# A fused mLSTM and mixture-of-experts kernel on one core: the state product behind the next scores, half-height products in runs of eight, gate products over 128 rows

## The chip, the core and the metric

The kernel runs on one core of a Trainium2 chip. The metric is device microseconds of one execution; the median of three runs of the kernel before is 420.7 us. TensorE (PE in the profile) multiplies, VectorE (DVE), ScalarE (ACT) and GpSimd (POOL) do the elementwise work, SyncE (SP) issues the transfers. PE writes only PSUM, which has eight banks of 128 x 512 floats.

## The reference, cut to what matters

```
for t in range(S):                       # mLSTM, B=2, H=8, S=768, D=40
    m_new  = maximum(f + m, i)
    f_stab, i_stab = exp(f + m - m_new), exp(i - m_new)
    C = f_stab * C + i_stab * outer(v_t, k_t)
    n = f_stab * n + i_stab * k_t
    y[t] = sigmoid(o_t) * (C @ q_t) / maximum(abs(n . q_t), 1)
x = y as (1536, 320)
for e in range(4):                       # experts, F=1024, dense
    out += p[:, e] * (relu(x @ w1[e]) @ w2[e])
```

## The kernel before, in words

The first part computes the mLSTM in chunks of 128 steps, six for each of the two batches, numbered n = 0 to 11. A chunk has these parts on PE: `inter` (product of the carried state with q; L458), `intra` (masked scores times values; L473, two 64-column products side by side), `state` (the chunk's own contribution to the carried state; L430, two 40-column products side by side, none in chunks 5 and 11), `scores` of the next chunk (L412, two products of at most 64 rows side by side), and `turn` (transposes of the result; L500). ACT scales the product of `inter` into `yb` (L465), DVE does `norm` (L486 to L493), the state's sum (L440), `weigh` (L418) and the decay scans (L385), POOL scales keys and values and the carried state (L396, L401, L446). Between these parts the loop issues `steps` of expert 0 as fillers: a step is a block of layer 1 (L147) or one output block of layer 2 (L178 to L180) with its eviction (L183 on ACT, L185 on DVE from expert 1 on).

The tiles `y1` (inter), `y0` (intra), `st` (state) and `px` (turn) all come from the pool `ps_y` with two banks, in this order, so `st` takes the bank of `y1` once `yb` has read it.

The gates are prepared in the first 30 us. Three of their products have fewer than 128 rows: `gate_t` (L298, 48 rows), `gate_l` (L320, 16 rows) and `spread` (L368, 48 rows).

Experts 1 to 3 then run in three groups of 512 tokens each, nine groups in all. A group has eight blocks of layer 1 (seven products of 128 rows each, plus one product of 64 rows, L170) and four outputs of layer 2 (24 products each). The products of 64 rows are done in pairs, one on each half of PE's rows, four at a time: `corners` is called at f0 = 0 and f0 = 4 and opens four banks, taken in turn from six (`ps_l` four, `ps_h` two); the two banks of `ps_o` hold the outputs.

Nothing reorders the program: each engine runs its instructions in the order in which the code issues them.

Of the kernel before, what the change touches and what calls it, by code (L numbers as in the profile page):

```python
# [18 lines left out]
L = 128  # L19
# [10 lines left out]

TERMS = ((0, 0), (0, 3), (3, 0), (1, 1), (1, 4), (4, 1), (2, 2), (2, 5))

QUAD = 4
KX, KW = 5, 6
C = 64
WARM = 4
# [7 lines left out]
def tile_mlstm_moe(ctx, tc, gt, qk, vk, ot, dp, w1, w2, out):  # L44
# [58 lines left out]
        split_hi(ws[:, HI, f], raw[:, f])  # L103
        split_lo(ws[:, LO, f], ws[:, HI, f], raw[:, f], eng)

    xd, banks = [], []

    def next_bank():

        i = len(banks) % 6  # L110
        p, tag = (ps_l, "pl") if i < 4 else (ps_h, "ph")
        banks.append(p.tile([L, 1, 512], F32, tag=tag, name="ph"))
        return banks[-1]

    class Expert:


        def __init__(self, e, t0, n, w1s, w2s):
            self.e, self.t0, self.n, self.w1s, self.w2s = e, t0, n, w1s, w2s
            self.nf = 512 // n  # L120
            self.hs = []
            self.nh, self.no = NF // self.nf, n // L
            self.i = 0
            self.quad = []

        def step(self):
            i = self.i
# [7 lines left out]
        def hidden(self, f0):  # L135
            n, nf = self.n, self.nf
            terms = TERMS
            if self.e:
                if not self.quad:
                    self.corners(f0)  # L140
                ph, terms = self.quad.pop(0), TERMS[:-1]
            else:
                ph = ps_h.tile([L, nf, n], F32, tag="ph", name="ph")
            for i in range(nf):
                f = f0 + i
                for k, (xi, wi) in enumerate(terms):
                    nc.tensor.matmul(  # L147
                        ph[:, i, :],
                        self.w1s[:, wi, f * L:(f + 1) * L],
                        xst[:, xi, self.t0:self.t0 + n],  # L150
                        start=(k == 0 and not self.e),
                        stop=(k == len(terms) - 1),
                    )
            h = hps[-1].tile([L, 2, nf, n], F32R, tag="h", name="h")
            hh, hl = h[:, HI], h[:, LO]
            nc.scalar.activation(hh, ph, AF.Relu)  # L156
            nc.vector.scalar_tensor_tensor(  # L157
                out=hl, in0=ph, scalar=0.0, in1=hh.bitcast(F32), op0=ALU.max, op1=ALU.subtract
            )
            self.hs += [(hh[:, i, :], hl[:, i, :]) for i in range(nf)]  # L160

        def corners(self, f0):

            t = slice(self.t0, self.t0 + self.n)
            self.quad = [next_bank() for _ in range(QUAD)]
            for i, ph in enumerate(self.quad):
                f = slice((f0 + i) * L, (f0 + i + 1) * L)
                r = slice(C * (i % 2), C * (i % 2) + C)
                x = xd[0][r, t] if i % 2 else xst[r, 2, t]
                nc.tensor.matmul(ph[:, 0, :], self.w1s[r, 5, f], x, start=True, stop=False)  # L170

        def output(self, t):
            e, ws = self.e, self.w2s
# [19 lines left out]
    with ExitStack() as actx:  # L193
# [37 lines left out]
        fs = gp.tile([BH, S], F32, name="fs")  # L231
        bs = gp.tile([BH, NC, L], F32, name="bs")

        ib = gp.tile([48, S], F32, name="ib")
        fr = a1.tile([48, NPE * L], F32R, name="fr")
        f_d = dram.tile([BH, S], F32, name="f_d")
        ident = const.tile([L, L], F32, name="ident")
        id4 = const.tile([L, 4, L], F32, name="id4")
# [1 line left out]

        bl = const.tile([L, NC, B * NP], F32, name="bl")

        sel = const.tile([48, BH], F32R, name="sel")

        par = gp.tile([BH, 2], F32, name="par")
        even = gp.tile([BH, 2, 64], F32, name="even")
        pair = gp.tile([BH, B * NP], F32, name="pair")
        fc = fs.rearrange("p (c t) -> p c t", t=L)

# [41 lines left out]
        def gate_t(c0, c1):  # L291

            pit = pits[c0] = ps_y.tile([L, 512], F32, tag="y", name="pit")
            n = c1 - c0
            po = n * 48
            for c in range(c0, c1):
                o = (c - c0) * 48
                nc.tensor.matmul(  # L298
                    pit[:, o:o + 48], ib[:, c * L:(c + 1) * L], ident[0:48, 0:48],
                    start=True, stop=True,  # L300
                )
            nc.scalar.activation(
                ibT[:, c0:c1], pit[:, 0:po].rearrange("t (c g) -> t c g", c=n), AF.Copy
            )

        def gate_last(c0, c1):
            n, m = c1 - c0, B * NP
            last = lasts[c0] = gp.tile([BH, m, n], F32, tag=f"last{c0}", name="last")
            nc.gpsimd.tensor_mul(
                last, pair.unsqueeze(2).to_broadcast([BH, m, n]),  # L310
                gat[:, 0].rearrange("p (c t) -> p c t", t=L)[:, c0:c1, L - 1].unsqueeze(1)
                .to_broadcast([BH, m, n]),
            )
# [48 lines left out]

        def spread(n, pool, tag):

            b, c = n // NC, n % NC
            fbs[n] = [pool.tile([L, 4, L], F32, tag=tag, name="fb") for _ in range(2)]
            for h in range(H):
                nc.tensor.matmul(  # L368
                    fbs[n][h // 4][:, h % 4, :],
                    sel[:, b * H + h:b * H + h + 1].to_broadcast([48, L]),  # L370
                    fr[:, c * L:(c + 1) * L], start=True, stop=True,
                )

        def load_f(n):
# [45 lines left out]
        def state(n, pool=ps_y, tag="y"):  # L420

            c, vv, kk = n % NC, vvs[n], kp[n % 2]
            if c == NC - 1:
                return
            st = pool.tile([L, NP, L], F32, tag=tag, name="st")
            blocks = [(slice(64 * r, 64 * r + D), slice(64 * r, 64 * r + D + 1)) for r in range(2)]
            for p in range(NP):
                for r, (q, q2) in enumerate(blocks):
                    h = 2 * p + r
                    nc.tensor.matmul(  # L430
                        st[q, p, q2], kk[:, h, 0:D], vv[:, h, 0:D + 1], start=True, stop=True
                    )
            cout = cs[(c + 1) % 2]
            if c == 0:
                for q, q2 in blocks:
                    copy(nc.scalar, cout[q, :, q2], st[q, :, q2])
            else:
                cd = cds.pop(n)
                for q, q2 in blocks:
                    nc.vector.tensor_add(cout[q, :, q2], cd[q, :, q2], st[q, :, q2])  # L440
# [89 lines left out]
        load_w1(1)  # L530
        make_identity(nc, ident)
        nc.gpsimd.memset(ib, 0.0)
        for t in vp + kp:
            nc.gpsimd.memset(t, 0.0)
        nc.vector.memset(mb[:, 0:1], -1e30)
# [1 line left out]
        nc.vector.memset(bs, 0.0)  # L537
        for t in cs:
            nc.vector.memset(t, 0.0)
        nc.vector.tensor_add(sel, ident[0:48, 0:BH], ident[0:48, 32:32 + BH])  # L540
        nc.scalar.activation(id4, ident.unsqueeze(1).to_broadcast([L, 4, L]), AF.Copy)
        heads = ident[0:BH, 0:BH].rearrange("k (i r) -> k i r", r=2)
        nc.vector.tensor_reduce(
            out=par.unsqueeze(2), in_=heads.rearrange("k i r -> k r i"),
            axis=mybir.AxisListType.X, op=ALU.add,
        )
        nc.scalar.activation(even, par.unsqueeze(2).to_broadcast([BH, 2, 64]), AF.Copy)
        nc.vector.tensor_add(pair, heads[:, :, 0], heads[:, :, 1])
        gate_max(0, 2)
        gate_f(0, 2, nc.vector)  # L550
        gate_i(0, 2, nc.vector)
# [72 lines left out]
        for n in range(2, NCH):  # L624
            j, cc = n // 2, n % 2
            k = SLOTS[n - 2]
            nxt = n + 1 < NCH
            if cc == 0 and j + 1 < NG:
                load_qk(j + 1)
                load_vk(j + 1)  # L630
            if NPE < n + 2 < NCH:
                load_f(n + 2)
            if cc == 0:
                if j > 1:
                    gate_o(j)
                if j + 1 < NG:
                    load_o(j + 1)
            if nxt:
                decay(n + 1)
            steps(k[0])  # L640
            if n == 2:
                quarter_hi(2)
                quarter_lo(2)
            inter(n)
            if n == 3:
                weights_out(4, nc.gpsimd)
            intra(n)
            state(n)
            norm(n)
            if n == 2:  # L650
                quarter_hi(3)
                quarter_lo(3)
            if nxt:
                scores(n + 1)
                values(n + 1)
                keys(n + 1)
                weigh(n + 1)
                carry(n + 1)
            steps(k[1])
            if cc == 0:  # L660
                steps(k[2])
            turn(n)
            turn_lo(n)
            if cc == 1:
                steps(k[2])
            if n == 2:
                weights_out(0, nc.vector)

                psum_e = const.tile([L, NCH, 1], F32, name="psum_e")
                nc.vector.tensor_reduce(out=psum_e, in_=pw, axis=mybir.AxisListType.X, op=ALU.add)  # L670
                nc.vector.tensor_scalar_add(psum_e, psum_e, 1e-9)
                nc.vector.reciprocal(psum_e, psum_e)
                nc.vector.tensor_mul(pw, pw, psum_e.to_broadcast([L, NCH, NE]))
# [108 lines left out]
```

## Time and profile before

| | |
|---|---|
| median of 3 runs | 420.7 us (420.6 to 420.71) |
| the profiled execution's own time | 420.61 us |
| span of its instructions | 418.8 us |
| PE busy | 408.6 us (98% of the span) |
| PEld (weight loads) busy | 364.7 us (87%) |
| DVE / ACT / POOL busy | 178.9 / 125.0 / 81.0 us |
| chain that ended last | PE 91%, ACT 3%, DVE 2%, POOL 2% |

A row of the timeline gives the start in us, the time from its first start to its last end, the engine, the line, output <- inputs, the shapes and the count of merged instructions; in brackets stands the idle time before it and what ended it. PE records overlap (a product's record lasts longer than the distance to the next), so distances are taken from start to start. An fp32 product appears as two weight loads and two passes.

### The profile page before, as it was taken

Reading aid. Unit: us, or ns where it says so; the run is one execution under the profiler, and the core shown is the slowest. Engines: PE = TensorE matmul, PEld = TensorE weight load, DVE = VectorE, ACT = ScalarE, POOL = GpSimd, SP = SyncE. Lnnn points to the kernel's source line nnn. Section 1 sums busy time; section 2 is a strip of 40 time slices with the busy share of each in tenths; the row PEclk is TensorE's granted clock in tenths of the full one; section 3 lists DMA queues with packets and bytes.
Section 4 is the critical chain, followed back from the end, with each engine's and each line's share of the span. In section 5 each row is a group of like instructions: output and inputs, shape, how many; then the busy total and the mean of one; then the engine's idle time right before and its main releaser. Section 6 shows DMA issues by size and latency. Waiting matters only on the chain.

```text
span 418.8 us, 7140 instructions
## 1 busy us (share of the span) xinstructions
PE 408.6 (98%) x3026; PEld 364.7 (87%) x3026; DVE 178.9 (43%) x321; ACT 125.0 (30%) x298; POOL 81.0 (19%) x92
## 2 busy tenths in 40 slices
PE   9898999999999999999999999999999999999996
PEld 5698899988899997997987978979979879789796
DVE  8969778575846213313223133132142341231321
ACT  5666223433343434205113042043130230220210
POOL 6865601222200441103310010015100000000000
PEclk9999999999999999999999999999999999999999
DMA  7988617276000030400300004003000000001001
GB/s 202 273 276 217 183 52 205 74 188 239 2 2 2 2 125 2 150 2 0 127 0 2 0 2 150 2 2 113 13 0 2 0 2 36 28 0 49 16 16 49
DMA packets 15080, 29.34 MB, mean 70 GB/s; under 512 B 1000, under 2 KB 10728, under 8 KB 13736
## 3 DMA queue, kind: packets, MB, share of 16 engines
q1 hardware_dynamic: 15048, 28.88, 22.6%
q8 instruction: 24, 0.39, 0.4%
q14 instruction: 8, 0.07, 0.0%
HBM read 26.86 MB, written 2.02 MB: 69 GB/s over the span
## 4 chain that ended last, share of the span: by engine, by line
PE 91%; ACT 3%; DVE 2%; POOL 2%; issue 1%; POOLq 0%; ACTq 0%
PE ph L147 40%; PE po L178 13%; PE po L180 13%; PE po L179 13%; PE ph L170 3%; PE s L412 2%; PE y L473 2%; PE y L458 2%; PE st L430 1%; PE px L500 1%; POOL w2s L92 1%; ACT yb L465 1%; POOL w1s L92 0%; ACT L262 0%; ACT L358 0%
## 5 line engine op out<-in xcount | busy, mean ns | idle before, releaser
L147 PE MATMUL ph<-xst,w1s 128*128 128x512 f32 (+1 forms) x888 | 171.1, 349 | 0.0
L147 PEld LDWEIGHTS ph<-xst,w1s 128*128 128x128 f32 x888 | 140.2, 189 | 27.8 <-issue 6.6
L178 PE MATMUL po<-w2s,h 128*128 128x320 f32 x384 | 119.6, 311 | 0.2 <-POOL w2s L92 0.2
L156 ACT ACTIVATE h<-ph 128x512 fp32r<-128x512 f32 x96 | 57.4, 598 | 205.6 <-PE ph L147 205.0
L180 PE MATMUL po<-w2s,h 128*128 128x320 f32 x384 | 118.6, 309 | 0.0
L179 PE MATMUL po<-w2s,h 128*128 128x320 f32 x384 | 118.6, 309 | 0.0
L157 DVE SCALAR_TENSOR_TENSOR h<-ph,h 128x512 fp32r<-128x512 f32 x96 | 66.2, 690 | 116.2 <-ACT h L156 115.8
L178 PEld LDWEIGHTS po<-w2s,h 128*128 128x128 f32 x384 | 72.1, 188 | 1.4 <-POOL w2s L92 0.5
L179 PEld LDWEIGHTS po<-w2s,h 128*128 128x128 f32 x384 | 72.1, 188 | 0.4
L180 PEld LDWEIGHTS po<-w2s,h 128*128 128x128 f32 x384 | 72.1, 188 | 0.0
L185 DVE SCALAR_TENSOR_TENSOR acc<-po,pw,acc 128x320 f32<-128x320 f32 x36 | 19.8, 550 | 100.0 <-PE po L180 100.0
L92 POOL TENSOR_TENSOR w1s<-raw,w1s 128x512 fp32r<-128x512 f32 (+1 forms) x24 | 23.6, 1017 | 58.2 <-ACT w1s L89 58.2
L92 POOL TENSOR_TENSOR w2s<-raw,w2s 128x640 fp32r<-128x640 f32 x6 | 9.4, 1571 | 104.0 <-ACT w2s L89 104.0
L385 DVE TENSOR_TENSOR_SCAN dd<-fb,id 128x512 f32<-128x512 f32 x24 | 29.4, 1264 | 0.2
L183 ACT ACTIVATE acc<-po,pw 128x320 f32<-128x320 f32 x12 | 6.3, 528 | 43.1 <-PE po L180 43.1
L465 ACT ACTIVATE yb<-y,ibT 128x41 f32<-128x41 f32 x80 | 16.0, 311 | 3.9 <-PE y L458 3.9
L418 DVE TENSOR_TENSOR pm<-s,dd 128x512 f32<-128x512 f32 x24 | 15.4, 682 | 0.2
L401 POOL TENSOR_TENSOR kp<-vk,dd 128x320 f32<-128x320 f32 x10 | 7.4, 737 | 38.1 <-DVE dd L385 38.1
L473 PE MATMUL y<-vp,pm 128*64 128x41 f32 x384 | 13.8, 231 | 0.7 <-DVE xst L508 0.7
L412 PE MATMUL s<-qk 64*128 64x128 f32 (+1 forms) x192 | 14.1, 284 | 0.2 <-DVE pm L418 0.2
L473 PEld LDWEIGHTS y<-vp,pm 128*64 128x64 f32 x384 | 12.3, 138 | 2.2 <-issue 0.8
L89 ACT ACTIVATE w2s<-raw 128x640 fp32r<-128x640 f32 x12 | 8.8, 732 | 15.9 <-DMA raw<-in_w 15.9
(94 smaller groups left out, 252.5 us busy)
## 6 DMA issues: line engine op xcount, KB each, us to landing
raw<-in_w SPq DMA_DIRECT2D x3, 1536.0 KB, 6.9
fb<-f_d SPq DMA_DIRECT2D x8, 512.0 KB, 7.2
raw<-in_w SPq DMA_DIRECT2D x3, 1280.0 KB
qk<-in_qk SPq DMA_DIRECT2D x4, 832.0 KB
vk<-in_vk SPq DMA_DIRECT2D x4, 640.0 KB, 8.1
acc<-in_ot SPq DMA_DIRECT2D x6, 320.0 KB, 10.8
out<-acc SPq DMA_DIRECT2D x12, 160.0 KB, 1.8
qk<-in_qk SPq DMA_DIRECT2D x4, 416.0 KB
```

The source lines that it names most:

```text
L92: eng.tensor_sub(lo, raw, hi.bitcast(F32))
L147: nc.tensor.matmul(ph[:, i, :], self.w1s[:, wi, f * L:(f + 1) * L], xst[:, xi, self.t0:self.t0 + n], start=(k == 0 and not self.e), stop=( ...
L156: nc.scalar.activation(hh, ph, AF.Relu)
L157: nc.vector.scalar_tensor_tensor(out=hl, in0=ph, scalar=0.0, in1=hh.bitcast(F32), op0=ALU.max, op1=ALU.subtract)
L178: nc.tensor.matmul(po, hh[:, sl], ws[:, LO, f, :], start=(f == 0), stop=False)
L179: nc.tensor.matmul(po, hh[:, sl], ws[:, HI, f, :], start=False, stop=False)
L180: nc.tensor.matmul(po, hl[:, sl], ws[:, HI, f, :], start=False, stop=(f == NF - 1))
L185: nc.vector.scalar_tensor_tensor(out=acc[:, i, :], in0=po, scalar=pw[:, i, e:e + 1], in1=acc[:, i, :], op0=ALU.mult, op1=ALU.add,)
L385: nc.vector.tensor_tensor_scan(out=dds[n][:, 4 * i:4 * i + 4].rearrange("p h t -> p (h t)"), data0=fbs[n][i].rearrange("p h t -> p (h t)") ...
L412: nc.tensor.matmul(ss[n][r][:, p, :], kg[q, p], qg[q, p], start=True, stop=True)
L465: nc.scalar.activation(yb[:, h], y1[:, h, 0:D + 1], AF.Copy, scale=ibT[:, c, i:i + 1])
L473: nc.tensor.matmul(y[t, h, 0:D + 1], pms[n][:, h, t], vvs[n][:, h, 0:D + 1], start=True, stop=True,)
```

## The change

Three things change.

1. In the loop over chunks 2 to 10, `state(n)` is issued behind `norm(n)` and `scores(n + 1)` in place of ahead of them.
2. `corners` is called once a group. It opens eight banks (two of `ps_o`, four of `ps_l`, two of `ps_h`) and issues all eight products of 64 rows, blocks 2 to 7 first and blocks 0 and 1, which lie in the banks of `ps_o`, last.
3. `gate_t`, `gate_l` and the spreads of chunks 2 and 3 read 128 rows; the added rows are zero. The tiles `ib`, `fr`, `sel`, `par`, `even` and `last` are made 128 rows high, and two small clears of `last` on POOL are added.

```
-    def next_bank():
-        i = len(banks) % 6
-        p, tag = (ps_l, "pl") if i < 4 else (ps_h, "ph")
-        banks.append(p.tile([L, 1, 512], F32, tag=tag, name="ph"))
-        return banks[-1]
+    def hidden_banks():
+        pools = [(ps_o, "po")] * 2 + [(ps_l, "pl")] * 4 + [(ps_h, "ph")] * 2
+        return [p.tile([L, 1, 512], F32, tag=tag, name="ph") for p, tag in pools]
...
-                if not self.quad:
-                    self.corners(f0)
-                ph, terms = self.quad.pop(0), TERMS[:-1]
+                if f0 == 0:
+                    self.corners()
+                ph, terms = self.banks[f0], TERMS[:-1]
...
-        def corners(self, f0):
+        def corners(self):
             t = slice(self.t0, self.t0 + self.n)
-            self.quad = [next_bank() for _ in range(QUAD)]
-            for i, ph in enumerate(self.quad):
-                f = slice((f0 + i) * L, (f0 + i + 1) * L)
-                r = slice(C * (i % 2), C * (i % 2) + C)
-                x = xd[0][r, t] if i % 2 else xst[r, 2, t]
-                nc.tensor.matmul(ph[:, 0, :], self.w1s[r, 5, f], x, start=True, stop=False)
+            self.banks = hidden_banks()
+            for f in (2, 3, 4, 5, 6, 7, 0, 1):
+                r = slice(C * (f % 2), C * (f % 2) + C)
+                x = xd[0][r, t] if f % 2 else xst[r, 2, t]
+                nc.tensor.matmul(
+                    self.banks[f][:, 0, :], self.w1s[r, 5, f * L:(f + 1) * L], x,
+                    start=True, stop=False,
+                )
...
-        ib = gp.tile([48, S], F32, name="ib")
-        fr = a1.tile([48, NPE * L], F32R, name="fr")
+        ib = gp.tile([L, S], F32, name="ib")
+        fr = a1.tile([L, NPE * L], F32R, name="fr")
...
-                    pit[:, o:o + 48], ib[:, c * L:(c + 1) * L], ident[0:48, 0:48],
+                    pit[:, o:o + 48], ib[:, c * L:(c + 1) * L], ident[:, 0:48],
...
-            b, c = n // NC, n % NC
+            b, c, k = n // NC, n % NC, 48 if n < 2 else L
...
-                    sel[:, b * H + h:b * H + h + 1].to_broadcast([48, L]),
-                    fr[:, c * L:(c + 1) * L], start=True, stop=True,
+                    sel[0:k, b * H + h:b * H + h + 1].to_broadcast([k, L]),
+                    fr[0:k, c * L:(c + 1) * L], start=True, stop=True,
...
+        for c0, c1 in ((0, 2), (2, NC)):
+            lasts[c0] = gp.tile([L, B * NP, c1 - c0], F32, tag=f"last{c0}", name="last")
+            nc.gpsimd.memset(lasts[c0], 0.0)
...
             intra(n)
-            state(n)
             norm(n)
...
             if nxt:
                 scores(n + 1)
+            state(n)
+            if nxt:
                 values(n + 1)
```

On PE, in chunk 3 (`y` of L458 is inter, `y` of L473 intra, `st` the state, `s` the next scores, `po` an output of expert 0), the order before was:

```order
L458 MATMUL y_627<-cs_129,qk_131 128x128 x4
L473 MATMUL y_645<-vp_125,pm 64x41 x16
L430 MATMUL st<-vp_125,kp_127 40x41 x8
L412 MATMUL s<-qk_130 128x128 x8
L178 MATMUL po<-w2s_93,h 128x320
```

With the change the same place reads as follows; the lines are numbered one lower.

```order
L457 MATMUL y_629<-cs_129,qk_131 128x128 x4
L472 MATMUL y_647<-vp_125,pm 64x41 x16
L411 MATMUL s<-qk_130 128x128 x8
L429 MATMUL st<-vp_125,kp_127 40x41 x8
L177 MATMUL po<-w2s_93,h 128x320
```

The eight products of the state and the eight of the scores have changed places.

On DVE, in chunk 2 (`dd` the decay scan, `cs` the state's sum, `y`, `nq`, `xr` the norm, `pm` the weigh), the order before was:

```order
L385 SCALAR_TENSOR_TENSOR dd<-fb,id_117 128x512 x2
L440 TENSOR_TENSOR cs_129<-cd,st 40x4x41 x2
L486 TENSOR_TENSOR y_507<-y_507,yb 128x8x41
L487 TENSOR_SCALAR nq<-y_507 128x8
L490 TENSOR_TENSOR xr<-y_507,acc 128x320
L491 TENSOR_TENSOR y_507<-y_507,nq 128x8
L492 RECIPROCAL y_507<-y_507 128x8
L493 TENSOR_TENSOR xr<-xr,y_507 128x320
L418 TENSOR_TENSOR pm<-s,dd 128x4x128 x2
```

With the change it is:

```order
L384 SCALAR_TENSOR_TENSOR dd<-fb,id_117 128x512 x2
L485 TENSOR_TENSOR y_509<-y_509,yb 128x8x41
L486 TENSOR_SCALAR nq<-y_509 128x8
L489 TENSOR_TENSOR xr<-y_509,acc 128x320
L490 TENSOR_TENSOR y_509<-y_509,nq 128x8
L491 RECIPROCAL y_509<-y_509 128x8
L492 TENSOR_TENSOR xr<-xr,y_509 128x320
L439 TENSOR_TENSOR cs_129<-cd,st 40x4x41 x2
L417 TENSOR_TENSOR pm<-s,dd 128x4x128 x2
```

The state's two sums have moved behind the norm.

On PE, at the start of expert 1's last two groups (numbers tell the banks apart), the order before was:

```order
L180 MATMUL po_2237<-w2s1_1904,h_2156 128x320
L170 MATMUL ph_2267<-xst_78,w1s1_1903 128x512
L170 MATMUL ph_2268<-xd_1896,w1s1_1903 128x512
L170 MATMUL ph_2269<-xst_78,w1s1_1903 128x512
L170 MATMUL ph_2270<-xd_1896,w1s1_1903 128x512
L147 MATMUL ph_2267<-xst_78,w1s1_1903 128x512 x7
L147 MATMUL ph_2268<-xst_78,w1s1_1903 128x512 x7
L147 MATMUL ph_2269<-xst_78,w1s1_1903 128x512 x7
L147 MATMUL ph_2270<-xst_78,w1s1_1903 128x512 x7
L170 MATMUL ph_2319<-xst_78,w1s1_1903 128x512
L170 MATMUL ph_2320<-xd_1896,w1s1_1903 128x512
```

With the change it is:

```order
L179 MATMUL po_2239<-w2s1_1906,h_2158 128x320
L166 MATMUL ph_2271<-xst_78,w1s1_1905 128x512
L166 MATMUL ph_2272<-xd_1898,w1s1_1905 128x512
L166 MATMUL ph_2273<-xst_78,w1s1_1905 128x512
L166 MATMUL ph_2274<-xd_1898,w1s1_1905 128x512
L166 MATMUL ph_2275<-xst_78,w1s1_1905 128x512
L166 MATMUL ph_2276<-xd_1898,w1s1_1905 128x512
L166 MATMUL ph_2269<-xst_78,w1s1_1905 128x512
L166 MATMUL ph_2270<-xd_1898,w1s1_1905 128x512
L144 MATMUL ph_2269<-xst_78,w1s1_1905 128x512 x7
L144 MATMUL ph_2270<-xst_78,w1s1_1905 128x512 x7
```

The second set of four has moved up into the run at the group's start; the last pair of the run writes the two banks that held the outputs before.

## Rows read from the trace of the kernel before

**Rows 1.** The page: busy time of each engine (share of the span) and instructions.

```profile
PE 408.6 (98%) x3026; PEld 364.7 (87%) x3026; DVE 178.9 (43%) x321; ACT 125.0 (30%) x298; POOL 81.0 (19%) x92
```

**Rows 2.** The waits of PE: engine, line, releaser, us in total, times, longest.

```profile
PE st L430 <- issue: 3.4, 5, 0.7
PE po L178 <- POOL w2s L92: 0.2, 1, 0.2
```

**Rows 3.** Timeline of PE and ACT in chunk 7.

```profile
85.07 1.13 PE L473 MATMUL y<-vp,pm 128*64 128x41 f32 x32
85.18 1.60 ACT L465 ACTIVATE yb<-y,ibT 128x41 f32<-128x41 f32 x8 [0.30 <-PE y L458]
86.88 0.51 PE L430 MATMUL st<-vp,kp 128*40 128x41 f32 x16 [0.68 <-issue]
87.32 1.16 PE L412 MATMUL s<-qk 64*128 64x128 f32 x16
88.41 0.41 PE L178 MATMUL po<-w2s,h 128*128 128x320 f32 x1
```

**Rows 4.** Timeline of PE in chunks 5 and 6.

```profile
63.81 1.13 PE L473 MATMUL y<-vp,pm 128*64 128x41 f32 x32
64.87 1.16 PE L412 MATMUL s<-qk 64*128 64x128 f32 x16
...
75.45 1.13 PE L473 MATMUL y<-vp,pm 128*64 128x41 f32 x32
...
77.92 0.39 PE L147 MATMUL ph<-xst,w1s 128*128 128x256 f32 x1
```

**Rows 5.** Timeline of PE in chunk 4.

```profile
51.82 1.13 PE L473 MATMUL y<-vp,pm 128*64 128x41 f32 x32 [0.67 <-DVE xst L508]
...
54.63 0.38 PE L147 MATMUL ph<-xst,w1s 128*128 128x256 f32 x1
```

**Rows 6.** Timeline of PE from the gates' last products to the end of chunk 2.

```profile
22.52 2.18 PE L147 MATMUL ph<-xst,w1s 128*128 128x256 f32 x16
24.62 1.09 PE L298 MATMUL pit<-ident,ib 48*128 48x48 f32 x8
...
27.75 0.40 PE L320 MATMUL pit<-last,even 16*128 16x32 f32 x2
...
30.21 1.30 PE L473 MATMUL y<-vp,pm 128*64 128x41 f32 x32
...
33.54 2.18 PE L147 MATMUL ph<-xst,w1s 128*128 128x256 f32 x16
35.56 0.52 PE L500 MATMUL px<-ident,xr 128*128 128x128 f32 x3
```

**Rows 7.** Timeline of DVE and POOL between 28 and 46 us.

```profile
28.55 0.69 DVE L157 SCALAR_TENSOR_TENSOR h<-ph,h 128x512 fp32r<-128x512 f32 x1 [2.25 <-ACT h L156]
29.15 1.28 DVE L418 TENSOR_TENSOR pm<-s,dd 128x512 f32<-128x512 f32 x2
...
41.22 3.99 POOL L92 TENSOR_TENSOR w2s<-w2r,w2s 128x640 fp32r<-128x640 f32 x2 [4.37 <-ACT w2s L89]
```

**Rows 8.** Timeline of PE and DVE where a group starts.

```profile
214.28 0.31 PE L180 MATMUL po<-w2s,h 128*128 128x320 f32 x1
214.51 0.50 PE L170 MATMUL ph<-xst,w1s 64*128 64x512 f32 x1
214.62 0.55 DVE L185 SCALAR_TENSOR_TENSOR acc<-po,pw,acc 128x320 f32<-128x320 f32 x1 [2.97 <-PE po L180]
```

**Rows 9.** Timeline of PE where a group's second four stand.

```profile
220.65 1.32 PE L147 MATMUL ph<-xst,w1s 128*128 128x512 f32 x5
221.91 0.50 PE L170 MATMUL ph<-xst,w1s 64*128 64x512 f32 x1
222.25 0.39 PE L170 MATMUL ph<-xst,w1s 64*128 64x512 f32 x1
222.57 1.66 PE L147 MATMUL ph<-xst,w1s 128*128 128x512 f32 x6
```

More of the change, by code (lines that the diff above doesn't have):

```diff
@@ L31 @@
 TERMS = ((0, 0), (0, 3), (3, 0), (1, 1), (1, 4), (4, 1), (2, 2), (2, 5))
-QUAD = 4
 KX, KW = 5, 6
@@ L104, in split_w2 @@
         split_lo(ws[:, LO, f], ws[:, HI, f], raw[:, f], eng)
-    xd, banks = [], []
-    def next_bank():
-        i = len(banks) % 6
-        p, tag = (ps_l, "pl") if i < 4 else (ps_h, "ph")
-        banks.append(p.tile([L, 1, 512], F32, tag=tag, name="ph"))
-        return banks[-1]
+    xd = []
+    def hidden_banks():
+        pools = [(ps_o, "po")] * 2 + [(ps_l, "pl")] * 4 + [(ps_h, "ph")] * 2
+        return [p.tile([L, 1, 512], F32, tag=tag, name="ph") for p, tag in pools]
     class Expert:
@@ L123, in __init__ @@
             self.i = 0
-            self.quad = []
+            self.banks = []
         def step(self):
@@ L241, in tile_mlstm_moe @@
         bl = const.tile([L, NC, B * NP], F32, name="bl")
-        sel = const.tile([48, BH], F32R, name="sel")
-        par = gp.tile([BH, 2], F32, name="par")
-        even = gp.tile([BH, 2, 64], F32, name="even")
+        sel = const.tile([L, BH], F32R, name="sel")
+        par = gp.tile([L, 2], F32, name="par")
+        even = gp.tile([L, 2, 64], F32, name="even")
         pair = gp.tile([BH, B * NP], F32, name="pair")
@@ L307, in gate_last @@
             n, m = c1 - c0, B * NP
-            last = lasts[c0] = gp.tile([BH, m, n], F32, tag=f"last{c0}", name="last")
+            last = lasts[c0]
             nc.gpsimd.tensor_mul(
-                last, pair.unsqueeze(2).to_broadcast([BH, m, n]),
+                last[0:BH], pair.unsqueeze(2).to_broadcast([BH, m, n]),
                 gat[:, 0].rearrange("p (c t) -> p c t", t=L)[:, c0:c1, L - 1].unsqueeze(1)
@@ L539, in tile_mlstm_moe @@
             nc.vector.memset(t, 0.0)
-        nc.vector.tensor_add(sel, ident[0:48, 0:BH], ident[0:48, 32:32 + BH])
+        nc.vector.tensor_add(sel, ident[:, 0:BH], ident[:, 32:32 + BH])
         nc.scalar.activation(id4, ident.unsqueeze(1).to_broadcast([L, 4, L]), AF.Copy)
-        heads = ident[0:BH, 0:BH].rearrange("k (i r) -> k i r", r=2)
+        heads = ident[:, 0:BH].rearrange("k (i r) -> k i r", r=2)
         nc.vector.tensor_reduce(
@@ L546, in tile_mlstm_moe @@
         )
-        nc.scalar.activation(even, par.unsqueeze(2).to_broadcast([BH, 2, 64]), AF.Copy)
-        nc.vector.tensor_add(pair, heads[:, :, 0], heads[:, :, 1])
+        nc.scalar.activation(even, par.unsqueeze(2).to_broadcast([L, 2, 64]), AF.Copy)
+        nc.vector.tensor_add(pair, heads[0:BH, :, 0], heads[0:BH, :, 1])
         gate_max(0, 2)
```

## The prediction

> **What bounds the kernel now.** I read the page first: PE is busy in 408.6 of the span's 418.8 us [rows 1], so PE's stream is the bound nearly everywhere, and a gain must be idle time of PE or time in which PE counts as busy without streaming. The list of waits comes second: the one large wait of PE inside the stream is that of the state, 3.4 us in five waits of 0.7 at most, put down to "issue", that is to nothing the list can name [rows 2]. The timeline names it. In chunk 7 the products of intra start at 85.07 and the state at 86.88. ACT's eight scalings into yb run from 85.18 to 85.18 + 1.60 = 86.78, and the state starts 0.10 later [rows 3]. The state's tile takes the bank that yb reads, so I take yb for the releaser. In chunk 5, which has no state, the scores start 1.06 after intra without waiting [rows 4].
>
> The records hide a second cost. Where PE goes from 128-row products to a pair of 64-row ones and back, it shows as busy, but the distances are longer. In layer 1 the plain step is (1.32 - 0.39)/4 = 0.2325 us from start to start: five products, of which a late one lasts about 0.39. The last plain product therefore starts at 220.65 + 1.32 - 0.39 = 221.58, the first pair 0.33 later, the second pair 0.34 after that, the first plain product 0.32 after that, and (1.66 - 0.39) - 4 x 0.2325 = 0.34 pass until the next [rows 9]. Each of these four distances is 0.09 to 0.11 over the plain step. I read the long step at a change of row height as about 0.09 for letting the stream run out and 0.105 for a weight load that nothing covers.
>
> **The change part by part.** The sum is made against the profiled execution: 420.61 us, span 418.8, so 1.8 lie outside the span; it stands 0.09 under the median of 420.7.
>
> *State behind the scores.* From intra's start to what follows the chunk's products, chunk 7 takes 88.41 - 85.07 = 3.34 now [rows 3], and chunks 2, 3, 8, 9 and 10 the same to 0.01 (chunk 2 has its ends in [rows 6]). Afterwards it is intra to scores 1.06 [rows 4], scores to the next 88.41 - 87.32 = 1.09, and state to the next 87.32 - 86.88 = 0.44 [rows 3]: 2.59. The bank is free at 86.78, while the state would now be due at 85.07 + 1.06 + 1.09 = 87.22, so 0.4 of cover is left. Each waiting chunk gains 0.75; four of them (7 to 10) give 3.00. Chunk 2 loses 0.18 of that: its intra lasts 1.30 and not 1.13 because it waits for the second half of weigh [rows 6], and this stays; it gives 0.57. Chunk 4 needs 54.63 - 51.82 = 2.81 now [rows 5] and gains 0.22. Chunk 6 has no inter and no wait: 77.92 - 75.45 = 2.47 becomes 2.59, a loss of 0.12 [rows 4]. That loss prices the order itself: intra and state share a form, and scores between them make one more change of form.
>
> Chunk 3 is counted at nothing. Its next step is the first output of expert 0, and PE already waits there for POOL's split of the second-layer weights [rows 2], which ends at 41.22 + 3.99 = 45.21 [rows 7]. That split follows ACT's half of it, which stands behind yb of chunk 3 on ACT. So what is gained before chunk 3 moves it, and what chunk 3 gains becomes wait. If POOL keeps up after all, 0.75 more is gained.
>
> On DVE the state's sum moves behind the norm, about 1.5 us later; behind it stand weigh and POOL's scaling of the carried state, and the next inter waits for it. At least two steps of expert 0, some 2 us each [rows 6], or one and a turn lie in between, and weigh itself stays where it was, so I cost this at nothing; without that cover it costs at most the 1.5 us in a chunk.
>
> *Gate products over 128 rows.* Weight loads are equally long, so only the changes of height go. From 22.52 to 27.75 PE does two steps of expert 0 and gate_t, 5.23 us. The step at 33.54, entered from another form and left without a change, takes 2.02, and eight passes of gate_t take 8 x (1.09 - 0.27)/7 = 0.94 with 0.27 for one late record [rows 6]. 2 x 2.02 + 0.94 = 4.98, a gain of 0.25 to 0.3; I take 0.3. Gate_l and spread lose similar seams between 27.75 and 30.21, but there intra of chunk 2 waits for weigh, which ends at 29.15 + 1.28 = 30.43 and stands on DVE behind h, which waits for ACT and so for the step before [rows 7]; only the 0.3 passes. Bounds: 0 and 0.7. Before 20 us PE waits for DVE, ACT and POOL, and the two small clears lie on a POOL that waits for DVE then: nothing.
>
> *Runs of eight.* Per group one entry and one exit go: 0.33 + 0.34 + 0.32 + 0.34 - 4 x 0.2325 = 0.40, the two moved pairs being counted at the plain step of 0.2325. Nine groups: 3.6. No row shows a third pair. Between the plain step and the 0.34 of the only two pairs in a row, I take the plain one, because the 0.105 in the 0.34 is the run's first load, and the second pair's is already covered. At 0.34 the term falls by 9 x 2 x 0.1075 = 1.9.
>
> The run's last pair writes the banks of the last two outputs. The last output's final product starts at 214.28, its eviction runs from 214.62 to 215.17, and the first pair starts at 214.51 [rows 8]. With a hand-over of 0.07 to 0.1 as in [rows 3] and 0.105 for the load, the fourth pair can stream at about 215.36, against 214.51 + 0.34 + 2 x 0.2325 = 215.32 unhindered: 0.04 a group, 0.35 in all. Bounds: nothing, and 0.2 a group. The run needs all first-layer weights of an expert at its start; they are split a group earlier.
>
> The Trainium skill says (TensorEngine Tiling (Array Packing), Key Properties) that a change of tiling mode drains TensorE, which speaks for the longer runs and against scores between intra and state. By the drain alone the time would be the 415.4 worked out among the rivals; the rows show a load's 0.105 beside it.
>
> **Sum.** 3.00 + 0.57 + 0.22 - 0.12 + 0.3 + 3.6 - 0.35 = 7.22. 420.61 - 7.22 = **413.4 us**, 1.7% under the median.
>
> **The rivals.**
> *The long run pays back.* Pairs in a run keep 0.34, or the last pair waits 0.2 a group: 415.0 to 416.6 (with both 1.9 and 1.5 back; the case in which only the 0.09 of each seam goes, 9 x 0.18 = 1.6, gives 413.4 + 2.0 = 415.4 and is counted here). For it: no third pair is on record, and the margin before the last pair is negative. Against it: the second pair's load shows covered.
> *More than forecast.* Chunk 3's 0.75 and the rest of the gates' 0.4 survive: 412.3. For it: POOL's 3.99 for two instructions includes time beside a DVE scan. Against it: the wait is there now.
> *The state's wait is another one.* If what ends it is not yb but something that moves with the state, the chunks gain nothing and all eight states pay 0.12 for the seam: 420.61 - 0.3 - 3.25 + 8 x 0.12 = 418.0. Against it: the 0.10 after yb's end, and chunk 6, which has no inter and no wait.
> *Slower.* All eight banks are open at the group's start, so the last pair hangs on the last output's eviction. If that came late by x each time, it costs 9x, and from x = (7.22 + 0.84)/9 = 0.9 us on the kernel is slower by over 0.2%. DVE would have to be occupied at each group's end; but L185 shows 2.97 idle before it [rows 8]. At x = 1 the time is 422.4. The Trainium skill warns of this (TensorEngine Tiling (Array Packing), Gotcha 1: PSUM Pressure): row tiles need banks of their own.
>
> **How the numbers follow.** Forecast (412.8 to 414.2) 0.66; the long run pays back 0.15; more than forecast 0.10; the state's wait is another one 0.05; slower 0.02; no change 0.02. The range takes in more than forecast and most of the payback: 412.2 to 415.8. A measurement here tells 0.2% (0.84 us) from no change: faster 0.95, same 0.02, slower 0.03.
>
> **What would show it.** Right: the wait of the state gone from PE's list, about 2.6 us from intra to the next step in chunks 7 to 10, nine runs of four pairs at 0.23 to 0.25, a longer wait for POOL's split near 44. Wrong: pairs at 0.34, a gap before the run's fourth pair, a wait before the state that outlasts the scores, or a new wait of inter for the state's sum.

## The result, and the profile after

The changed kernel takes 413.8 us (median; 413.78 to 413.82). Against the kernel before, run beside it (420.69 us), the ratio is 0.9837, with a 95% interval of 0.9819 to 0.9854: 1.6% less, and clear of no change. It is 0.4 us above the forecast of 413.4. The profiled execution took 413.80 us with a span of 412.0; before, 420.61. The sum of the prediction was 7.22 and the measured difference is 6.81. In some executions of these kernels the granted clock lies at half for a few us near 21 us and the time is about 1.5 us longer; the times and readings below are taken from executions, or from stretches of one, without that.

The page's row of engines answers to [rows 1]. PE is busy 4.6 us less and its weight loads 2.1 more; the other engines hold the same work to 0.6.

```profile
PE 404.0 (98%) x3026; PEld 366.8 (89%) x3026; DVE 178.7 (43%) x321; ACT 124.9 (30%) x298; POOL 81.6 (20%) x94
```

The waits of PE (engine, line, releaser, us in total, times, longest) answer to [rows 2]. The state's 3.4 us are gone, and POOL's split of the second-layer weights has grown from 0.2 to 1.3.

```profile
PE po L177 <- POOL w2s L91: 1.3, 1, 1.3
```

The timeline of PE and ACT in chunk 7 answers to [rows 3].

```profile
84.74 1.13 PE L472 MATMUL y<-vp,pm 128*64 128x41 f32 x32
84.85 1.59 ACT L464 ACTIVATE yb<-y,ibT 128x41 f32<-128x41 f32 x8 [0.30 <-PE y L457]
85.80 1.16 PE L411 MATMUL s<-qk 64*128 64x128 f32 x16
...
86.89 0.51 PE L429 MATMUL st<-vp,kp 128*40 128x41 f32 x16
87.33 0.41 PE L177 MATMUL po<-w2s,h 128*128 128x320 f32 x1
```

`yb` ends at 84.85 + 1.59 = 86.44, the state starts at 86.89, 0.45 after it. From intra to what follows the chunk it is 87.33 - 84.74 = 2.59, as forecast; before it was 3.34.

Where the time came from is read best from the start of `inter` in each chunk, since everything ahead of it is contained in it. Chunk 6 has no inter. The last column is what was gained since the row above.

| start of | before | after | gained | since the row above |
|---|---|---|---|---|
| inter, chunk 3 | 37.82 | 36.87 | 0.95 | gates and chunk 2: 0.95 |
| inter, chunk 4 | 50.10 | 49.66 | 0.44 | chunk 3: -0.51 |
| inter, chunk 5 | 62.82 | 62.37 | 0.45 | chunk 4: 0.01 |
| inter, chunk 7 | 84.09 | 83.75 | 0.34 | chunks 5 and 6: -0.11 |
| inter, chunk 8 | 97.79 | 96.71 | 1.08 | chunk 7: 0.74 |
| inter, chunk 11 | 132.47 | 129.14 | 3.33 | chunks 8 to 10: 2.25 |
| first product of 64 rows | 156.81 | 153.48 | 3.33 | chunk 11: 0 |
| last eviction | 415.67 | 408.85 | 6.82 | the nine groups: 3.49 |

Two rows differ from the forecast in kind: chunk 3 took back part of what came to it, and chunk 4 gained nothing.

**Chunk 3.** The timeline of DVE, POOL and PE there, with the single instructions ([rows 7] has the two splits in one row). DVE's scans are those of `decay(4)`.

```profile
39.78 1.22 DVE L384 TENSOR_TENSOR_SCAN dd<-fb,id 128x512 f32<-128x512 f32 x1
40.26 2.10 POOL L91 TENSOR_TENSOR w2s<-w2r,w2s 128x640 fp32r<-128x640 f32 x1 [4.17 <-ACT w2s L88]
40.92 2.52 DVE L384 TENSOR_TENSOR_SCAN dd<-fb,id 128x512 f32<-128x512 f32 x1
42.32 2.46 POOL L91 TENSOR_TENSOR w2s<-w2r,w2s 128x640 fp32r<-128x640 f32 x1
...
44.83 0.42 PE L177 MATMUL po<-w2s,h 128*128 128x320 f32 x1 [1.26 <-POOL w2s L91]
```

In the kernel before the same four read as follows.

```profile
40.17 1.22 DVE L385 TENSOR_TENSOR_SCAN dd<-fb,id 128x512 f32<-128x512 f32 x1
41.22 1.55 POOL L92 TENSOR_TENSOR w2s<-w2r,w2s 128x640 fp32r<-128x640 f32 x1 [4.37 <-ACT w2s L89]
41.31 2.55 DVE L385 TENSOR_TENSOR_SCAN dd<-fb,id 128x512 f32<-128x512 f32 x1
...
42.72 2.49 POOL L92 TENSOR_TENSOR w2s<-w2r,w2s 128x640 fp32r<-128x640 f32 x1
```

The reader is to see how the ends follow each other. A scan lasts 1.22 and a split 1.55 to 1.58 where nothing lies beside them. After, scan 1 ends at 41.00 and split 1, though recorded from 40.26, ends 1.36 later, at 42.36. Scan 2 ends at 43.44, 1.08 after that, and split 2 at 44.78, 1.34 after that. The four take turns: each ends after the one ahead of it on the other engine by its length alone less 0.1 to 0.2. Before, split 1 came only 0.17 before scan 1 ended and lost nothing; the rest of the turns is the same (42.77, 43.86, 45.21). So split 2 hangs on scan 1, that is on DVE. The timeline marks no gap on DVE from 28.8 to 47 us in the changed kernel, and its scan came only 0.39 earlier (40.17 to 39.78) while POOL's first split came 0.96 earlier (41.22 to 40.26). PE waits for split 2, which ended 0.43 earlier, and that is all that reached chunk 4.

The Trainium skill (SBUF — State Buffer, Who interferes with whom) says that a VectorE instruction with two inputs in SBUF contends with a GpSimd instruction that reads SBUF, that the port pair which the two share is an exclusive lock, and, of VectorE's two-port modes, that whoever issues first has the pair for the whole instruction while the other blocks. The scans of `decay(4)` read the transfer's `fb` and a constant, both in SBUF, and the splits read SBUF, so the first of these covers them; these rows agree in order and in length, and show the turn by whole instructions for a scan too. If the two only shared a bandwidth, I would expect both to stretch at once and not their ends to follow in turn; that is argued and not run. Chunk 2 has the other case: the scans of `decay(3)` read `fb` from PSUM, where the spread's product left it.

```profile
30.02 2.33 DVE L384 TENSOR_TENSOR_SCAN dd<-fb,id 128x512 f32<-128x512 f32 x2
30.63 0.72 POOL L91 TENSOR_TENSOR w1s<-wb,w1s 64x256 fp32r<-64x256 f32 x1
31.72 1.27 POOL L91 TENSOR_TENSOR w1s<-wa,w1s 128x512 fp32r<-128x512 f32 x1 [0.36 <-ACT w1s L88]
```

There the two scans take 2.33, as alone, and the two splits of the first-layer weights take 0.72 and 1.27, against 0.72 and 1.26 for the shortest of their kind in the kernel.

**Chunk 4.** PE and DVE there, after; L154 is the eviction `h` that frees the bank for the third step of expert 0.

```profile
53.98 6.32 PE L144 MATMUL ph<-xst,w1s 128*128 128x256 f32 x48
...
56.17 1.29 DVE L417 TENSOR_TENSOR pm<-s,dd 128x512 f32<-128x512 f32 x2
...
57.38 0.68 DVE L154 SCALAR_TENSOR_TENSOR h<-ph,h 128x512 fp32r<-128x512 f32 x1
58.12 1.01 PEld L144 LDWEIGHTS ph<-xst,w1s 128*128 128x128 f32 x8 [0.25 <-DVE h L154]
```

The weight load of the third step waits for `h`, which ends at 58.06. `h` stands behind weigh on DVE, in a row of instructions that starts at 50.52 (50.95 before) and has no gap. The three steps take 6.32 where they took 6.12, and the 0.22 of [rows 5] is gone there. The row of before:

```profile
54.63 6.12 PE L147 MATMUL ph<-xst,w1s 128*128 128x256 f32 x48
```

**The runs of eight.** PE, its loads and DVE where a group starts, which answers to [rows 8]; of each pair one record is shown.

```profile
210.18 0.31 PE L179 MATMUL po<-w2s,h 128*128 128x320 f32 x1
...
210.42 0.50 PE L166 MATMUL ph<-xst,w1s 64*128 64x512 f32 x1
...
210.53 0.55 DVE L184 SCALAR_TENSOR_TENSOR acc<-po,pw,acc 128x320 f32<-128x320 f32 x1 [2.97 <-PE po L179]
...
210.76 0.40 PE L166 MATMUL ph<-xst,w1s 64*128 64x512 f32 x1
...
211.00 0.39 PE L166 MATMUL ph<-xst,w1s 64*128 64x512 f32 x1
...
211.13 0.18 PEld L166 LDWEIGHTS ph<-xd,w1s 64*128 64x128 f32 x1
...
211.23 0.39 PE L166 MATMUL ph<-xst,w1s 64*128 64x512 f32 x1
```

The pairs start 0.34, 0.24 and 0.23 apart: the first distance holds the first load, the others stream. The last output's eviction ends at 211.08, the load for the last pair starts at 211.13, and its product is on time. The chain shows the groups; its rows give the start, the length and the count.

```profile
182.01 1.13 PE ph L166 x6
...
210.49 1.13 PE ph L166 x5
```

From run to run 28.48 pass, and all nine runs last 1.12 to 1.14. Before, the same chain has at these places

```profile
185.73 0.66 PE ph L170 x3
...
214.59 0.66 PE ph L170 x3
```

which are 28.86 apart.

### The profile page after: what moved, and what is told of

It reads as the page before. It is cut to its first block, busy times and chain, and to the rows that moved or that the text cites. A ratio compares the mean times of both kernels' runs of the same rounds, so it can differ in the third digit from the quotient of the medians.

```text
span 412.0 us, 7144 instructions
## 1 busy us (share of the span) xinstructions
PE 404.0 (98%) x3026; PEld 366.8 (89%) x3026; DVE 178.7 (43%) x321; ACT 124.9 (30%) x298; POOL 81.6 (20%) x94
## 4 chain that ended last, share of the span: by engine, by line
PE 92%; ACT 3%; DVE 3%; POOL 1%; issue 1%; ACTq 0%
PE ph L144 40%; PE po L177 14%; PE po L179 13%; PE po L178 13%; PE ph L166 2%; PE s L411 2%; PE y L472 2%; PE y L457 2%; PE px L499 1%; PE st L429 1%; ACT yb L464 1%; POOL w2s L91 1%; ACT L261 0%; ACT L357 0%; DVE pm L417 0%
## 5 line engine op out<-in xcount | busy, mean ns | idle before, releaser
L144 PE MATMUL ph<-xst,w1s 128*128 128x512 f32 (+1 forms) x888 | 168.8, 348 | 0.0
L154 DVE SCALAR_TENSOR_TENSOR h<-ph,h 128x512 fp32r<-128x512 f32 x96 | 66.3, 690 | 112.3 <-ACT h L153 111.9
```

The costliest lines, as they stand in the source:

```text
L144: nc.tensor.matmul(ph[:, i, :], self.w1s[:, wi, f * L:(f + 1) * L], xst[:, xi, self.t0:self.t0 + n], start=(k == 0 and not self.e), stop=( ...
L154: nc.vector.scalar_tensor_tensor(out=hl, in0=ph, scalar=0.0, in1=hh.bitcast(F32), op0=ALU.max, op1=ALU.subtract)
```

## The experiments

**One part at a time.** Three kernels are the kernel before with one part of the change: the move of `state(n)` behind `scores(n + 1)`, the runs of eight, the gate products over 128 rows. The edits are the change's own; the first is

```
             intra(n)
-            state(n)
             norm(n)
...
                 scores(n + 1)
+            state(n)
+            if nxt:
                 values(n + 1)
```

> The kernel before with the state behind norm and scores alone. Theory (the wait is that for yb, and POOL's split of second-layer weights is slowed by the decay scan that DVE does beside it): chunks 7 to 10 gain 0.75 each and chunk 6 loses 0.12, as in the changed kernel. Without the gates' part DVE is not moved at all, so POOL's two split instructions start 0.57 earlier, overlap the scan longer and end where they ended, near 45.2; chunk 4 gains nothing because its third step waits for DVE. Sum 2.9: 417.8 us. Rival (POOL's split follows ACT alone and is not slowed): the 0.57 of chunk 2 and the 0.22 of chunk 4 are kept, 417.0 us, and the split ends at 44.6.

Measured: 417.61 us, ratio 0.9930 (0.9906 to 0.9953). Its profile is read by differences from start to start, from inter of chunk 2 on: chunk 2 gained 0.60, chunk 3 took back 0.51, chunk 4 gained 0.02, chunk 6 lost 0.11, chunks 7 to 10 gained 3.0. POOL's row is that of the whole change (4.52):

```profile
42.10 4.50 POOL L92 TENSOR_TENSOR w2s<-w2r,w2s 128x640 fp32r<-128x640 f32 x2 [3.74 <-ACT w2s L89]
```

PE waits 1.3 for it. So the 0.51 belongs to the move of the state, and neither to the gates nor to the runs.

> The kernel before with the runs of eight alone. Theory: each of nine groups loses two changes of row height, 0.385 to 0.40 as the groups of the changed kernel show, and nothing waits: 3.5 us, 417.2 us. Rival (part of the 3.5 came from the other edits, or the run waits for the eviction when the groups start later): 418 us or more.

Measured: 417.16 us, the median of the four executions at a mean clock of 0.999 or 1.0 (417.06 to 417.33); over all eight, up to 420.1, the median is 417.94 and the ratio 0.9938 (0.9917 to 0.9958). By those four the part is worth 420.65 - 417.16 = 3.5, and in its trace the nine groups are 3.43 shorter. The groups are 28.48 long as in the whole change, and the state's wait is still 3.4 us.

> The kernel before with the 128-row gate products alone. Theory: gate_t loses its two changes of height, 0.3; the seams of gate_l and spread go too, but intra of chunk 2 waits for weigh. DVE, ACT and POOL all move by 0.3 together, so the split is slowed as much as before and 0.3 reaches the end: 420.3 to 420.4 us. Rival (nothing reaches the end, the wait for POOL takes it): 420.65.

Measured: 420.19 us in one run, 0.42 to 0.46 under the kernel before. Inter of chunk 3 starts 0.39 earlier, and the end comes 0.42 earlier. The three parts, 3.04, 3.4 to 3.5 and 0.42 to 0.46, add to 6.9 or 7.0, against 6.89 between the medians of the whole change: to about 0.1 they do not help or hinder each other.

**The order of the eight.** The changed kernel with the blocks in natural order, so that the first pair of the run, not the last, writes the banks of the outputs.

```
-            for f in (2, 3, 4, 5, 6, 7, 0, 1):
+            for f in range(NF):
```

> The changed kernel with the eight products in the order of blocks 0 to 7, so that the first pair writes the two banks of the outputs. Theory: the first pair waits for the eviction of the last output, from 0.24 after that output's last product to 0.95 after it: 0.7 in each of nine groups, 6.3 us in all, 420.1 us, with a gap before every run of eight. Rival (the bank's hand-over costs little in any order): 413.8 to 414.5.

Measured: 420.14 us in one run. The same place as above reads

```profile
211.54 0.31 PE L179 MATMUL po<-w2s,h 128*128 128x320 f32 x1
...
211.89 0.55 DVE L184 SCALAR_TENSOR_TENSOR acc<-po,pw,acc 128x320 f32<-128x320 f32 x1 [2.97 <-PE po L179]
212.50 0.18 PEld L166 LDWEIGHTS ph<-xd,w1s 64*128 64x128 f32 x1 [0.53 <-DVE acc L184]
```

The load waits until 0.06 after the eviction's end at 212.44. A group is 28.84 to 29.20 long, 0.69 to 0.73 more than in the changed kernel. This is the mechanism of the rival "slower", made to happen: 9 x 0.70 = 6.3, nearly all that the change gives. PE's list of waits names only 1.8 us of it in eight waits, since the half product ahead counts as busy until 212.27:

```profile
PE ph L166 <- DVE acc L184: 1.8, 8, 0.2
```


**Another bank for the state.** The changed kernel with the state ahead of the scores again, as before, but in a bank of `ps_o`.

```
             intra(n)
+            state(n, ps_o, "po")
             norm(n)
...
-            state(n)
```

> The changed kernel with the state again ahead of norm and scores, but its tile in a bank of the outputs' pool, so that it doesn't wait for yb. Theory (yb's bank was the wait): no wait before the state, and intra, state and scores in the old order save the seam: a chunk takes 0.96 + 0.44 + 1.09 = 2.49 in place of 2.59, 0.10 less in chunks 7 to 10 and 0.12 in chunk 6, about 0.5 in all: 413.2 to 413.3 us. Rival (the wait was for something else that stands with the state, such as POOL's keys): 0.7 to 0.85 comes back in chunks 7 to 10, 416.5 us or more.

Measured: 413.3 us in one run. Chunk 7 in the old order:

```profile
84.68 1.13 PE L472 MATMUL y<-vp,pm 128*64 128x41 f32 x32
...
84.79 1.59 ACT L464 ACTIVATE yb<-y,ibT 128x41 f32<-128x41 f32 x8 [0.30 <-PE y L457]
...
85.63 0.48 PE L429 MATMUL st<-vp,kp 128*40 128x41 f32 x16
...
86.05 1.16 PE L411 MATMUL s<-qk 64*128 64x128 f32 x16
...
87.14 0.42 PE L177 MATMUL po<-w2s,h 128*128 128x320 f32 x1
```

The state starts 0.75 before `yb` ends (86.38), in the place where it used to wait. That shows what the profile before left as "issue": the wait was for the bank. The chunk takes 2.46 here and 2.59 in the changed kernel, so the old order is the shorter one once the bank is free, by 0.13 where chunk 6 had priced 0.12. Chunk 2 loses 0.56 instead: 0.28 by a wait of the state (I read it as the bank of `ps_o`, which the first scan of `decay(3)` reads until about 31.2; the list names POOL's split, which ends at 31.36, 0.02 before the state, but which the state does not read; that was not tried apart), the rest by the turn, whose norm stands behind the state's sum on DVE. Chunk 3's wait for POOL swallows it.

**The scan away from the split.** The changed kernel with `decay(4)` issued on DVE behind the state of chunk 3.

```
-            if nxt:
+            if nxt and n != 3:
                 decay(n + 1)
...
             state(n)
+            if n == 3:
+                decay(4)
```

> The changed kernel with the decay scans of chunk 4 issued behind the state of chunk 3, so that DVE does norm and not the scans while POOL splits the last second-layer weights of expert 0. Theory (the scan slows POOL's split): the two split instructions take 3.1 to 3.5 in place of 4.5, the 1.26 wait of PE for them falls to 0.3 or less, 412.6 to 412.9 us. Rival (any tensor work of DVE slows POOL as much, or POOL follows ACT alone): the split takes 4.2 or more and the time stays at 413.5 to 413.8.

Measured: 412.38 us in one run, 0.2 less than the least expected.

```profile
40.27 3.10 POOL L91 TENSOR_TENSOR w2s<-w2r,w2s 128x640 fp32r<-128x640 f32 x2 [4.19 <-ACT w2s L88]
...
43.05 1.39 DVE L384 TENSOR_TENSOR_SCAN dd<-fb,id 128x512 f32<-128x512 f32 x1
43.32 1.64 POOL L395 TENSOR_TENSOR vp<-vk,ibT 128x320 f32<-128x320 f32 x1
```

Both splits now take 3.10 together beside DVE's eviction, norm and sum, where they took 4.52 beside the scans; PE's wait for them is gone from its list and inter of chunk 4 starts at 48.25 and not at 49.66. The blocking has moved to `vp`, which lasts 1.64 and not 0.72 and ends at 44.96, 0.52 after the scan's end at 44.44; PE has no new wait for it.

**All together.** The old order in `ps_o`, the late decay, in chunk 4 weigh between the first and second step, and the transposes of chunk 3 in a bank of `ps_o`, so that intra of chunk 4 need not wait for their eviction. The first kernel has the old order in all chunks, the second keeps the changed kernel's order in chunks 2 and 3, and its edit is:

```
+            if n > 3:
+                state(n, ps_o, "po")
             norm(n)
...
+                if n < 4:
+                    state(n)
+                if n == 3:
+                    decay(4)
...
+            if n == 4:
+                steps(1)
+                weigh(n + 1)
+                steps(1)
...
+            if n == 3:
+                turn(n, ps_o, "po")
```

> The changed kernel with the state ahead of norm in an outputs' bank, the late scans of chunk 4, chunk 5's weigh behind one step of expert 0 in chunk 4, and chunk 3's transposes in an outputs' bank so that chunk 4's intra doesn't wait for their eviction. Theory: 0.5 (no seam) + 1.0 to 1.2 (POOL's wait) + 0.2 (DVE in chunk 4) + 0.67 (intra's wait in chunk 4) = 2.4 to 2.6 less than the changed kernel, 411.2 to 411.4 us. Rival (these waits hide one another and DVE, which has no gap from 28 to 48 us, bounds this stretch): 412.5 or more.

Measured: 411.81 us, ratio 0.9772 (0.9748 to 0.9796), 0.4 to 0.6 over what was expected. The 0.56 of chunk 2 came back (inter of chunk 3 at 37.43), since no wait for POOL swallowed it any longer. The transposes' bank did what was expected: intra's 0.67 is gone from the list, and from inter to inter chunk 4 takes 12.03 and not 12.71. But the third step there still waits for DVE, where two scans now take 2.82 and not 2.34:

```profile
31.39 0.51 PE L429 MATMUL st<-vp,kp 128*40 128x41 f32 x16 [0.21 <-POOL w1s L91]
...
50.45 2.82 DVE L384 TENSOR_TENSOR_SCAN dd<-fb,id 128x512 f32<-128x512 f32 x2
...
56.60 2.18 PE L144 MATMUL ph<-xst,w1s 128*128 128x256 f32 x16 [0.23 <-DVE h L154]
```

> As e8_combined, but with the state of chunks 2 and 3 behind the scores as in the changed kernel and only that of later chunks ahead of norm in an outputs' bank. Theory (in chunks 2 and 3 the state's bank in the outputs' pool is still held by the gates' spread, and the state's sum ahead of norm delays turn, which cost e5 and e8 0.56 at the start of chunk 3): that 0.56 comes back, of which DVE's order takes up to 0.3 in chunk 4: 411.1 to 411.5 us. Rival (DVE bounds chunks 3 and 4 in any order): 411.8 as e8.

Measured: 411.12 us (411.09 to 411.21), ratio 0.9767 (0.9749 to 0.9786), the fastest here, 2.7 us under the changed kernel. Inter of chunk 3 starts at 36.90, that of chunk 4 at 48.27 and that of chunk 5 at 60.30. The state's bank, the split and intra's wait are out of PE's list, which still has

```profile
PE px L499 <- DVE xr L492: 0.9, 1, 0.9
...
PE y L472 <- DVE pm L417: 0.3, 2, 0.2
...
PE ph L144 <- DVE h L154: 0.2, 1, 0.2
```

## Why the prediction was right, and where its sizes were off

The forecast named `yb`'s bank as the state's releaser, the seams between 128-row and 64-row products as the second cost, and a longer wait for POOL's split as the place where chunk 3's gain goes. All three are in the trace after, and 413.8 lies inside the likeliest case. That the total came within 0.4 is in part luck: chunks 3 and 4 gave 0.72 less than their terms, and the other terms together 0.32 more. Term by term (us gained, profiled executions):

| step of the sum | forecast | measured |
|---|---|---|
| gates and chunk 2 | 0.3 + 0.57 = 0.87 | 0.95 |
| chunk 3 | 0 | -0.51 |
| chunk 4 | 0.22 | 0.01 |
| chunk 6 | -0.12 | -0.11 |
| chunks 7 to 10 | 3.00 | 2.99 |
| runs of eight and their last pair | 3.6 - 0.35 = 3.25 | 3.49 |
| sum | 7.22 | 6.82 |

- *State behind the scores.* Chunks 7 to 10 came out to 0.01, and 0.45 of cover was left where 0.4 was forecast. That `yb` was the releaser is shown by the kernel with another bank. In chunk 2 the list of before puts the state's wait (0.5) down to POOL's split of the first-layer weights; the split had ended 0.32 before the state's start at 32.01, and `yb` 0.09 before it, as in the other chunks. The state's sum behind the norm cost nothing, as counted: the list after has no wait of inter for it.
- *Chunk 3 at nothing.* Mis-sized, and the largest miss: it took back 0.51. The step said that what is gained ahead moves ACT's half and so POOL's split; it did, by 0.96. It left out that POOL's second split ends a turn behind DVE's second scan, and that DVE, without a gap from 28.8 us on, came only 0.39 earlier. [rows 7] had the sign of it, 3.99 for two splits (1.55 + 2.49 in single rows), which the prediction used only for a gain. Late decay shows the cause: without the scans beside them the splits take 3.10.
- *Chunk 4's 0.22.* The step took PE's distance alone. The third step's bank is freed by DVE's `h` behind weigh, and "weigh itself stays where it was" was true and the reason: DVE gained 0.43 there, PE would have gained 0.22 more, and waits 0.25. The last two kernels move weigh behind the first `h` and still show 0.23, but they do not tell weigh's place from the rest of DVE's row: PE comes to the steps 0.67 earlier there, since intra no longer waits, and the scans take 0.48 more.
- *Gates.* The step's own rows give 0.25 (5.23 - 4.98), and 0.3 was taken. It is 0.39 at inter of chunk 3 in the kernel with gates alone; the 0.57 of chunk 2 measured 0.60 in the kernel with the state alone.
- *Runs of eight.* A group became 0.37 to 0.41 shorter, against 0.40 for the seams. The 0.35 charged for the last pair did not arise: the hand-over from DVE was 0.05 and not 0.07 to 0.1, and the load that follows it fits beside the third pair.
- *Rivals.* "The long run pays back": pairs stream at 0.23, and the last one is on time. Its upper end should read 413.4 + 1.9 + 1.5 = 416.8 and not 416.6, on which nothing hangs. The case in which only the 0.09 of each seam goes, 0.18 a group, is excluded by the 0.37 to 0.41; how the seam divides into a stream that runs out and a load was not measured apart. "The state's wait is another one": excluded by the other bank. "More than forecast": chunk 3 gave back 0.51 in place of gaining 0.75. "Slower": the mechanism is real, and only the order of the eight keeps it away; even at 0.70 a group it stays below the 0.9 from which it decides.

## What to carry to other kernels

When a wait is put down to nothing the list can name, look at which buffer the waiting tile inherits: here a bank still being read, and another bank or another order both cured it. Ask of a gain whether every engine behind it has idle time there: VectorE ran without a gap here, and what took turns with it (GpSimd's splits behind its scans) moved by what VectorE moved, not by what TensorE gained. When one long run opens all banks at once, give the banks freed last to its last products: that order was worth 6.3 us here.

## What the runs showed of the hardware that was not expected

- A scan on VectorE and an elementwise operation on GpSimd, both reading SBUF, excluded each other instruction by instruction: 1.22 became 2.52 and 1.55 became 2.46, while a scan that reads PSUM, and VectorE's eviction, norm and sum, cost GpSimd's splits nothing (0.72, 1.27, and 3.10 for two).
- The groups of expert 2 are shorter than those of experts 1 and 3 (28.14 against 28.48 after, 28.55 against 28.85 before). After, the difference lies in layer 1: its 56 products of 128 rows start within 12.6 us for expert 2 and 12.9 for the others, while the outputs are equal to 0.1. The shapes are the same; the weights of expert 2 lie in the buffers that expert 0 had, those of experts 1 and 3 in others. Whether that is the cause was not tried.
- TensorE's granted clock fell to half in some executions. The windows of 0.5 us of the kernel with the state alone (us; busy PE, loads, DVE, ACT, POOL; granted clock; DMA share, GB/s):

```profile
21.00:21.50 0.50, 0.50 (x7) 0.50 (x8) 0.12 (x1) 0.40 (x2) 0.27 (x2) 0.67 1.11 428
21.50:22.00 0.50, 0.50 (x8) 0.50 (x8) 0.33 (x1) 0.50 (x2) 0.00 (x0) 0.50 1.09 438
...
24.50:25.00 0.50, 0.50 (x6) 0.50 (x6) 0.50 (x1) 0.02 (x1) 0.00 (x0) 0.92 0.95 313
```

  The clock goes from 2.4 to 1.2 GHz in 21.0 to 21.5 and is back before 25. PE had been idle from 20.0 to 20.5 and busy from then on. It cost 1.49 us: inter of chunk 2, up to which the program is that of before, starts at 30.61 and not at 29.12. The changed kernel's profile has 1.00 there, with PE idle from 20.0 to 20.5 as well. What decides it was not tried.
